# Turning six of eight halves' key sums by transposing DMAs over 16-bit planes instead of TensorE transposes

## The chip, the cores and the metric

The kernel runs on one core of one Trainium2 chip. The metric is device microseconds of one execution, as the median of several runs. The profile is a separate execution that the hardware profiler recorded.

## What is computed

Attention with positive random features (a softmax-free form) feeds a mixture of experts with one expert per token:

```python
# q, k, v: 8 batches x 8 heads x 576 tokens x 64; omega: 128 features x 64
q_s, k_s = (q * scale, k * scale)
def phi(x):
    h = einsum('bhsd,md->bhsm', x, omega) - sum(x * x, -1) / 2
    return exp(h - max(h, -1)) / sqrt(m)
kv  = einsum('bhsm,bhsd->bhmd', phi(k_s), v)      # sums over the keys
num = einsum('bhsm,bhmd->bhsd', phi(q_s), kv)
den = einsum('bhsm,bhm->bhs', phi(q_s), z) + 1e-06   # z: sum of phi(k_s)
x = (num / den) as 4608 tokens x 512
logits = normalised(x) @ normalised(expert_emb).T / tau
expert_idx = argmax(logits)                        # 8 experts
out[token] = gate * (relu(x @ w1[e]) @ w2[e])      # 512 -> 1024 -> 512
```

## The kernel before

The first stage, up to some 200 us, makes the attention and sorts the tokens by expert; the second, TensorE back to back, runs the experts. The change lies in the first.

It is one loop with 45 turns `i` over 36 token tiles of 128 rows. A super-batch has nine tiles and holds two batches, so that the key sums are made in eight halves (sb, b): a half is complete in turn 5, 9, 14, 18, 23, 27, 32 or 36. The queries run `LAG` = 7 turns behind the keys (`iq = i - LAG`). TensorE's order in a turn with both: projection of the queries (L373), transposes of the previous tile's query features (`qtr`, L461, into `nuu`), projection of the keys (L373), first step of the key sums `kv(1)` (L405), numerators `num` (L481, into `nuu`), second step `kv(0)` (L405). In words of the rows: `kva` holds key sums in accumulation memory, `kvs` their copy, `vtNv` the values of tile N, `ftk` and `ftq` the features, `xgp` a buffer of the second stage that is free here and lent out.

The routing logits need each head's key sums times the expert embeddings, eight more columns of `kvs`, so the numerator matmul of a query gives its logits too. For that the key sums must be turned around. Two turns after a half is complete, in the turning turn `i + 2`, which is 11, 16, 20, 25, 29 or 34 for the six middle halves, this happens:

- `kv_dense` (L423), still in turn i: GpSimd copies `kvs` into a dense 128x512 in `xgp[2]` (`xgp[NPRE]`).
- `kv_turn` (L432): four TensorE transposes of it, behind `kv(1)`.
- `kv_turned` (L436): VectorE copies the result back to `xgp[2]`.
- `kv_logits` (L443): 16 small matmuls with the embeddings, behind `num`, ahead of `kv(0)`. They write a strip of `nuu`'s second bank.
- `kv_logits_out` (L449): VectorE copies that strip into `kvs`, behind the emptying of the numerators (`num_out`, L494 to L500: `rr`, `lg`, `xr`). The next turn's `qtr` writes `nuu` again.

ScalarE makes the features (L387), copies half of the transposed queries (L466) and the key sums (L419). GpSimd does small steps of the routing (L520 to L593; from L589 on those that choose the first expert) and scatters finished tiles to memory with an indirect DMA (L569), one after the other. SP issues the loads of keys (L342), values (L357), queries (L363) and, from turn 29 on, of the first expert's weights (L601), and waits for buffers in that order. VectorE's and ScalarE's order is the order in which the code is written, by `todo` lists for named places in a turn; the other engines follow the scheduler's order.

Of the kernel before, what the change touches and what calls it, by code (L numbers as in the profile page):

```python
# [15 lines left out]
U16 = mybir.dt.uint16  # L16
# [7 lines left out]
B, H, S, D, M = 8, 8, 576, 64, 128  # L24
E, F = 8, 1024
N = B * S
DM = H * D
# [12 lines left out]
NPRE = 2  # L40
# [24 lines left out]
def attention_moe(ctx: ExitStack, tc: tile.TileContext, qT, kT, v1, omT, emb, tau, w1q, w2q, xs, out):  # L65
    nc = tc.nc
# [57 lines left out]
    xgp = [const.tile([P, PAY], F32, name=f"xgp{t}") for t in range(NPRE + 1)]  # L124
# [134 lines left out]
    def flush():  # L259
        while lows:  # L260
            lows.pop(0)()
# [60 lines left out]
    with ExitStack() as c1:  # L322
# [5 lines left out]
        kva, kvs, st = {}, {}, {}  # L328
# [5 lines left out]
        def load(i):  # L334

            if i >= NTILE:
                return
            if i == LAG - 1:
                st["k", i] = xgp[0][:, 0:DM].rearrange("p (c m) -> p c m", c=4)
            else:  # L340
                st["k", i] = p1.tile([P, 4, P], F32, name=f"kt{i}", tag="qt" if i in (2, 3) else "kt", bufs=2)
            nc.sync.dma_start(st["k", i], kT[i])  # L342
# [47 lines left out]
        def kvmm(i, a, b):  # L390
            sb, u = divmod(i, TPS)
            ft = st["fk", i, a]
            vt = st["v0", i] if (u, b) == (4, 0) else st["v", i]
            begin = u == 4 * b
            if begin:
                if (sb, b) == (0, 0):
                    kva[0, 0, a] = nu[a][:, 0 : 4 * (D + 1)].rearrange("p (h d) -> p h d", h=4)
                else:
                    kva[sb, b, a] = ps.tile([P, 4, D + 1], F32, name=f"kva{sb}_{b}_{a}", tag=f"kv{a}")
            acc = kva[sb, b, a]  # L400
            for h in range(4):


                for c in range(0, P, 64):
                    nc.tensor.matmul(  # L405
                        acc[c : c + 64, h, :], ft[:, h, c : c + 64], vt[:, 2 * h + a, :],
                        start=begin and h == 0, stop=u == 4 + 4 * b and h == 3,
                    )
            if u == 4 + 4 * b:
                if a == 0:  # L410
                    kvs[sb, b] = p1.tile([P, H, D + 1 + E], F32, name=f"kvs{sb}_{b}", tag="kvs", bufs=2)
# [22 lines left out]
        def kv_turned(sb, b):  # L434
            kvt = xgp[NPRE][:, 0:DM].rearrange("p (c m) -> p c m", c=4)
            nc.vector.tensor_copy(kvt.rearrange("p c m -> p (c m)"), st["kvb"])  # L436
            st["kvt", sb, b] = kvt

        def kv_logits(sb, b):
            st["kve", sb, b] = pe = nu[1][:, 424 : 424 + 8 * E].rearrange("p (c e) -> p c e", c=4)  # L440
            for c in range(4):
                for o in range(0, P, 64):
                    nc.tensor.matmul(  # L443
                        pe[o : o + 64, c], st["kvt", sb, b][:, c, o : o + 64], enbd[:, c].rearrange("p a e -> p (a e)"),
                        start=True, stop=True,
                    )
# [148 lines left out]
        def first_weights(n):  # L595

            if n == 0:
                st["fe"] = nc.values_load(firsti[0:1, NPRE + 1 :], engines=[ET.SP], min_val=0, max_val=E - 1, skip_runtime_bounds_check_because=WHY)
            q, wn = n // 2, ("w1", "w2")[n % 2]
            st["rf", n] = raw = rawp.tile([P, F], F32, name=f"rf{n}", tag=f"raw_{wn}")  # L600
            nc.sync.dma_start(raw, W[wn][0].rearrange("(e q) p f -> e q p f", q=NQ)[ds(st["fe"], 1), q].rearrange("o p f -> (o p) f"))  # L601
# [124 lines left out]
        early, spare, mid, ends, behind = {}, {}, {}, {}, []  # L726
# [9 lines left out]
        def go(d, *key):  # L736
            for f, *a in d.pop(key, ()):
                f(*a)
# [7 lines left out]
        for i in range(NTILE + LAG + 2):  # L746
# [3 lines left out]
            ahead = i + (4 if i < 2 else 2)  # L750
            if i < 2 or i > 4:
                load(ahead)
            if i in LOADS:
                first_weights(LOADS[i])
            if i == 1 or i >= 4:
# [10 lines left out]
            ks, qs = i < NTILE, 0 <= iq < NTILE  # L766
            st["both"] = ks
            sb, u = divmod(i - 1, TPS)

            def kv(*halves, b=None):  # L770
                if 0 <= i - 1 < NTILE:
                    for a in halves:
                        kvmm(i - 1, a, int(u > 4) if b is None else b)
# [5 lines left out]
            if ks and qs:  # L779
                if i > LAG:  # L780
                    proj(q1 + (3,), q0 + (1,))
                if turns:
                    qtr(iq - 1, *nu)
                maxima(*q1)
                if turns:
                    qcopy(iq - 1, 1)
                    qcopy(iq - 1, 0, True)
                maxima(*q0)
                go(spare, i, 4)
                feats(*q1)  # L790
                feats(*q0)
                proj(k1 + (2,), k0 + (0,))
                maxima(*k1)
                maxima(*k0)
                kv(1)
                if u == 4:
                    kv(0)
                    kv_out(sb, 0)
                go(spare, i, 3)
                slot(4)  # L800
                if sums:
                    num(iq - 1)
                go(spare, i, 0)
                go(spare, i, 1)
                slot(2)
                if u == 4:
                    kv(0, 1, b=1)
                else:
                    kv(0)
                if sums:  # L810
                    num_out(iq - 1)
                feats(*k1)
                feats(*k0)
                slot(0)
                slot(1)
            elif ks:
                for j in KPROJ.get(i, ()):
                    proj(*keys(j))
                if i == LAG - 1:
                    proj(("q", 0, 1, 3), ("q", 0, 0, 1))  # L820
                go(spare, i, 0)
                maxima(*k0)
                maxima(*k1)
                slot(0)
                if i == LAG - 1:
                    kv_out(0, 0)
                    kv_dense(0, 0)
                    for a in range(2):
                        kvmm(i - 2, a, 1)
                    kv_turn(0, 0)  # L830
                    emb2()
                kv(0, 1)
                slot(1)
                feats(*k0)
                go(spare, i, 1)
                feats(*k1)
                slot(2)
            else:
                mine, other = ((3, 1), (0, 2))[:: 1 if i % 2 == NTILE % 2 else -1]
                if qs:  # L840
                    proj(q1 + (mine[0],), q0 + (mine[1],))
                kv(1)
                go(spare, i, 2)
                slot(3)
                if turns:
                    qtr(iq - 1, *(pb[k] for k in other))
                kv(0)
                if sums:
                    num(done)
                go(spare, i, 0)  # L850
                if i == NTILE + 1:
                    flush()
                if qs:
                    maxima(*q1)
                    maxima(*q0)
                if i > NTILE and turns:
                    qcopy(iq - 1, 0, True)
                if qs:
                    feats(*q1)
                if i == NTILE:  # L860
                    kv_out(sb, 1)
                    qcopy(iq - 1, 0, True)
                if qs:
                    feats(*q0)
                if turns:
                    qcopy(iq - 1, 1)
                if sums:
                    num_out(done)
                flush()
                filled(1)  # L870
                slot(0)
                slot(1)
                filled(FILLS[i] - 1)
                go(spare, i, 1)
                slot(2)
            if sums and done % G == G - 1:
# [16 lines left out]
                for n, (d, *key) in enumerate(plan):  # L893
                    todo = at(d, *key) if key[0] < NTILE + LAG + 2 else behind
                    todo.insert(0 if n == 0 else len(todo), (next, steps, None))
            go(ends, i)
            if 0 <= i - 1 < NTILE and u in (4, 8):
                b = u // 4 - 1
                if b and ks:
                    kv_out(sb, b)  # L900
                k = int(not ks)
                if i + 2 == LAG:
                    todo = (kv_turned, spare, i + 2, 4), (kv_logits, spare, i + 2, 3), (kv_logits_out, mid, i + 2, 4)
                else:
                    kv_dense(sb, b)
                    todo = (kv_turn, spare, i + 2, 3 - k), (kv_turned, mid, i + 2, 4 - k)
                    todo += (kv_logits, spare, i + 2 + k, 0), (kv_logits_out, mid, i + 2 + k, 0)
                for f, *key in todo:
                    at(*key).append((f, sb, b))
# [184 lines left out]
    with tc.manual_schedule(engines={ET.PE, ET.Activation, ET.DVE, ET.Pool, ET.SP}):  # L1094
# [82 lines left out]
        for t in range(NPRE, NSTAT):  # L1177
# [10 lines left out]
            early = late and (t < SHIFT or t == ends)  # L1188
# [105 lines left out]
    with tc.If(tot > NSTAT):  # L1294
        with tc.For_i(NSTAT, tot, 1) as i:
            get = lambda k, eng, mx: nc.values_load(tabi[k : k + 1, ds(i, 1)], engines=[eng], min_val=0, max_val=mx, skip_runtime_bounds_check_because=WHY)
            xgl = x_of("x", get(0, ET.SP, DUM))
            src = get(2, ET.SP, E * NQ - 1)
# [65 lines left out]
```

## Time and profile before

| what | value |
|---|---|
| median of 3 runs | 637.44 us (637.18 to 638.03) |
| profiled execution | 641.91 us, of it span 640.3 us |
| TensorE busy | 627.2 us, 98% of the span |
| VectorE, ScalarE, GpSimd busy | 491.8, 431.8, 420.6 us |
| granted clock | 0.998 |

A row of the trace has the start in us from the start of the span and the duration; times of groups on TensorE overlap by the length of the pipeline, so a group's place is best read from its start to that of the next. The profiled execution is one run; it is not the median.

### The profile page before, as it was taken

How to read it: one execution, taken by the hardware profiler on the slowest of the kernel's cores; microseconds unless marked ns; L12 is line 12 of the kernel's file. 1: busy time of each engine (PE TensorE's matmuls, PEld its weight loads, DVE VectorE, ACT ScalarE, POOL GpSimd, SP SyncE). 2: the span in 40 equal slices, each digit the busy share in tenths (PEclk: the TensorE clock that was granted, in tenths of full speed). 3: DMA queues.
4: the chain of work that ended last, by engine and by line, in shares of the span. 5: the costliest groups of instructions: out<-in, count | busy, mean ns of one | idle time of the engine just before them, and what ended most of it. 6: DMA issues, size and time to landing. Idle time of an engine off the chain costs nothing.

```text
span 640.3 us, 19056 instructions
## 1 busy us (share of the span) xinstructions
PE 627.2 (98%) x6289; PEld 535.4 (84%) x6290; DVE 491.8 (77%) x908; ACT 431.8 (67%) x1139; POOL 420.6 (66%) x603
## 2 busy tenths in 40 slices
PE   9999999999999899999999999999999999999996
PEld 8899999988888688888888888888888888888885
DVE  5688888898879755687778887787778786878754
ACT  6898898898988426755666675757565756666630
POOL 3012443355777644569789797979797979798852
PEclk9999999999999999999999999999999999999999
DMA  7655664767772277978877788686869686878631
GB/s 255 199 153 163 216 209 154 233 203 229 271 270 100 101 239 275 264 183 242 210 237 200 210 232 245 185 256 172 245 184 236 208 237 200 229 218 216 201 116 46
DMA packets 142239, 131.93 MB, mean 206 GB/s; under 512 B 106742, under 2 KB 106870, under 8 KB 142144
## 3 DMA queue, kind: packets, MB, share of 16 engines
q1 hardware_dynamic: 135520, 109.70, 59.7%
q0 software_dynamic: 6480, 20.91, 8.4%
q8 instruction: 57, 0.93, 0.6%
q14 instruction: 38, 0.31, 0.2%
q10 hardware_dynamic: 144, 0.07, 0.0%
HBM read 83.78 MB, written 21.97 MB: 165 GB/s over the span
## 4 chain that ended last, share of the span: by engine, by line
PE 70%; ACT 2%; DVE 1%; DMA 1%; issue 0%; POOL 0%; ACTq 0%
PE pb L284 31%; PE po L284 31%; PE fs_o L284 2%; PE pb L373 1%; PE nuu L481 1%; ACT ftq L387 1%; PE pb L266 1%; PE fs_a L284 1%; DMA rf<-w2q 1%; PE kva L405 1%; PE pb L461 0%; DVE nmq L377 0%; DVE xr L500 0%; PE nuu L538 0%; PE nuu L461 0%
## 5 line engine op out<-in xcount | busy, mean ns | idle before, releaser
L239 POOL TENSOR_TENSOR w2l<-raww,w2h 128x256 f32 x128 | 143.3, 1120 | 7.6
L239 POOL TENSOR_TENSOR w1l<-raww,w1h 128x256 f32 (+1 forms) x130 | 112.5, 865 | 14.5 <-DMA xgp<-xs 5.2
L284 PE MATMUL po<-w2h,hh 128*128 (+1 forms) x288 | 112.2, 390 | 0.0
L284 PE MATMUL po<-w2h,hl 128*128 (+1 forms) x288 | 112.1, 389 | 0.0
L284 PE MATMUL po<-w2l,hh 128*128 (+1 forms) x288 | 112.1, 389 | 0.0
L284 PE MATMUL pb<-w1h,xh 128*128 (+1 forms) x280 | 109.4, 391 | 0.0
L284 PE MATMUL pb<-w1h,xl 128*128 (+1 forms) x280 | 109.0, 389 | 0.0
L284 PE MATMUL pb<-w1l,xh 128*128 (+1 forms) x280 | 109.0, 389 | 0.0
L1084 DVE COPY pl<-pb 128x512 uint16<-128x512 uint16 x68 | 46.7, 689 | 60.2 <-ACT pl L1080 55.9
L1080 ACT ACTIVATE pl<-pb 128x512 uint16<-128x512 uint16 x68 | 39.4, 585 | 76.3 <-PE pb L284 66.5
L314 POOL DMA_INDIRECT y<-xgp,tail x36 | 45.0, 1250 | 55.2 <-DVE w1h L233 28.8
L387 ACT ACTIVATE ftq<-pb,nmq 128x128 f32<-128x128 f32 x288 | 79.6, 429 | 2.2 <-DVE nmq L377 1.3
L387 ACT ACTIVATE ftk<-pb,nmk 128x128 f32<-128x128 f32 x272 | 76.6, 479 | 6.0 <-DVE nmk L377 4.3
L1102 DVE COPY wd<-t 128x1024 uint16<-128x1024 uint16 x68 | 65.4, 963 | 1.6 <-DMA t<-pl 1.5
L1118 ACT ACTIVATE hh<-wd 128x1024 fp32r<-128x1024 f32 x34 | 36.1, 1063 | 42.7 <-DVE wd L1102 38.1
L284 PEld LDWEIGHTS po<-w2h,hh 128*128 128x128 f32 x288 | 54.1, 188 | 11.2
L284 PEld LDWEIGHTS po<-w2l,hh 128*128 128x128 f32 x288 | 54.1, 188 | 11.2
L284 PEld LDWEIGHTS po<-w2h,hl 128*128 128x128 f32 x288 | 54.0, 187 | 11.2
L284 PEld LDWEIGHTS pb<-w1h,xl 128*128 128x128 f32 x280 | 52.6, 188 | 11.0
L284 PEld LDWEIGHTS pb<-w1l,xh 128*128 128x128 f32 x280 | 52.6, 188 | 10.9
L284 PEld LDWEIGHTS pb<-w1h,xh 128*128 128x128 f32 x280 | 52.5, 187 | 10.7
L1122 DVE SCALAR_TENSOR_TENSOR hl<-wd,hh 128x1024 fp32r<-128x1024 f32 x34 | 54.2, 1594 | 4.0 <-ACT hh L1118 3.4
(341 smaller groups left out, 1250.4 us busy)
## 6 DMA issues: line engine op xcount, KB each, us to landing
raww<-w1q SPq DMA_DIRECT2D x38, 512.0 KB
raww<-w2q SPq DMA_DIRECT2D x38, 512.0 KB
qt<-qT SPq DMA_DIRECT2D x36, 256.0 KB
kt<-kT SPq DMA_DIRECT2D x35, 256.0 KB
xg<-xs SPq DMA_DIRECT2D x23, 260.5 KB
xgp<-xs SPq DMA_DIRECT2D x15, 260.5 KB
rf<-w1q SPq DMA_DIRECT2D x4, 512.0 KB
rf<-w2q SPq DMA_DIRECT2D x4, 512.0 KB
```

Source lines behind the costliest of these rows:

```text
L239: ils.append(eng.tensor_tensor(at(l, d)[:, c], raw[:, c], at(h, d)[:, c].bitcast(F32), op=ALU.subtract))
L266: nc.tensor.transpose(bank[:, c * P : (c + 1) * P], src[:, o + c * P : o + (c + 1) * P], ident)
L284: done.append(nc.tensor.matmul(dst, x[:, c * P : (c + 1) * P], ws.rearrange("p o f -> p (o f)"), start=(begin and i == 0 and k == 0), stop ...
L314: w = nc.gpsimd.indirect_dma_start(out=out, out_offset=bass.IndirectOffsetOnAxis(ap=(xg[:, DM:] if tail is None else tail)[:, E : E + 1].b ...
L373: nc.tensor.matmul(st["pj" + w, i, a][:, c, :], st[w, i][r, c, :], om[r, :], start=True, stop=True)
L387: nc.scalar.activation(ft[:, h, :], pj[:, h, :], AF.Exp, bias=nm[:, h : h + 1])
L405: nc.tensor.matmul(acc[c : c + 64, h, :], ft[:, h, c : c + 64], vt[:, 2 * h + a, :], start=begin and h == 0, stop=u == 4 + 4 * b and h == 3,)
L1080: nc.scalar.activation(planes[1][:, o : o + 512], halved(src)[:, :, 1], AF.Copy)
L1084: nc.vector.tensor_copy(planes[0][:, o : o + 512], halved(src)[:, :, 0])
L1102: nc.vector.tensor_copy(to, src)
L1118: nc.scalar.activation(hh, wd[:, 0:F], AF.Relu)
L1122: nc.vector.scalar_tensor_tensor(hl, wd[:, 0:F], 0.0, hh.bitcast(F32), op0=ALU.max, op1=ALU.subtract)
```

## The change

For the six middle halves, while keys are still loaded, the turn of the 32-bit sums is made from two 16-bit halves of each value. `kv_planes` lets GpSimd take `kvs` apart into two planes, low and high 16 bits, in `xgp[2]`, in turn i. `kv_spun` has SP issue two DMA transposes, one per plane, into `xgp[0]`, in turn i + 1, ahead of the values' load. `kv_joined` lets GpSimd join the planes to 32-bit values in `xgp[2]`, in turn i + 2. `kv_logits` goes to a new place, behind `kv(0)` and ahead of the emptying; `kv_logits_out` keeps its own. The first half and the last stay as they were. Lines of the changed kernel behind L438 are 18 higher.

```diff
+        def kv_planes(sb, b):
+            pl = xgp[NPRE][:, 0:DM].bitcast(U16).rearrange("p (k c a d) -> p k a c d", k=2, a=2, d=D)
+            src = kvs[sb, b].bitcast(U16).rearrange("p (a c) (w two) -> p a c w two", a=2, two=2)
+            for k in range(2):
+                nc.gpsimd.tensor_copy(pl[:, k], src[:, :, :, 0:D, k])
+
+        def kv_spun(sb, b):
+            pl = xgp[NPRE][:, 0:DM].bitcast(U16).rearrange("p (k f) -> p k f", k=2)
+            st["t16", sb, b] = xgp[0][:, 0:DM].bitcast(U16).rearrange("p (k c m) -> p k c m", k=2, c=4)
+            for k in range(2):
+                nc.sync.dma_start(st["t16", sb, b][:, k], pl[:, k], transpose=True)
+
+        def kv_joined(sb, b):
+            st["kvt", sb, b] = kvt = xgp[NPRE][:, 0:DM].rearrange("p (c m) -> p c m", c=4)
+            to = xgp[NPRE][:, 0:DM].bitcast(U16).rearrange("p (c m two) -> p c m two", c=4, two=2)
+            for k in range(2):
+                nc.gpsimd.tensor_copy(to[:, :, :, k], st["t16", sb, b][:, k])
+
@@
                 load(ahead)
+            go(early, i, "spin")
             if i in LOADS:
@@
                     kv(0)
+                go(spare, i, 2)
                 if sums:
@@
+                elif ks:
+                    kv_planes(sb, b)
+                    todo = (kv_spun, early, i + 1, "spin"), (kv_joined, mid, i + 2, 4)
+                    todo += (kv_logits, spare, i + 2, 2), (kv_logits_out, mid, i + 2, 0)
                 else:
                     kv_dense(sb, b)
```

TensorE at the end of turn 11, before: the transposes stand behind `kv(1)` (`vt10v` with the first feature half), the numerators repeat, and the logits stand ahead of `kv(0)`.

```order
L405 MATMUL kva_0_1_883<-vt10v,ftk_1_924 64x65 x8
L432 MATMUL pb_74<-ident,xgp_137 128x128 x4
L481 MATMUL nuu<-kvs_0_439,qp_0_976 64x73
...
L443 MATMUL nuu<-enbd,xgp_137 64x16 x8
L405 MATMUL kva_0_0_908<-vt10v,ftk_0_929 64x65 x8
L373 MATMUL pb_74<-om,qt_823 128x128
```

The same place in the changed program:

```order
L405 MATMUL kva_0_1_886<-vt10v,ftk_1_927 64x65 x8
L499 MATMUL nuu<-kvs_0_439,qp_0_979 64x73
...
L405 MATMUL kva_0_0_911<-vt10v,ftk_0_932 64x65 x8
L461 MATMUL nuu<-enbd,xgp_137 64x16 x8
L373 MATMUL pb_74<-om,qt_824 128x128
```

The transposes are gone, and the logits have gone from ahead of `kv(0)` to behind it, right ahead of the next turn's projection.

GpSimd from the end of turn 14 into turn 16, before (`xgp_137` is `xgp[2]`, L569 the scatter, L547 to L557 routing steps):

```order
L423 COPY xgp_137<-kvs_0_1392 128x2x4x64
L489 COPY xr_1555<-ids 128x1
L547 TENSOR_TENSOR base_1572<-base_1572,run 128x24
...
L557 TENSOR_TENSOR pos_1576<-pos_1576 128x3
L569 DMA xs<-xr_917,posi_1280 38016x576
L563 CAST posi_1681<-pos_1576 128x3
```

The same place in the changed program (`xgp_135` is `xgp[0]`):

```order
L443 COPY xgp_137<-kvs_0_1392 128x2x4x64 x2
L507 COPY xr_1558<-ids 128x1
L565 TENSOR_TENSOR base_1575<-base_1575,run 128x24
...
L575 TENSOR_TENSOR pos_1579<-pos_1579 128x3
L587 DMA xs<-xr_920,posi_1280 38016x576
L455 COPY xgp_137<-xgp_135 128x512 x2
L581 CAST posi_1673<-pos_1579 128x3
```

One copy has become two, and two joins stand behind the scatter of turn 16.

GpSimd in turn 29, before:

```order
L593 TENSOR_TENSOR keyc<-keyc,iote 128x8
L563 CAST posi_3251<-pos_3114 128x3
L520 TENSOR_TENSOR t_3255<-lg_2971 128x96
L521 TENSOR_TENSOR t_3255<-t_3255 128x3x16
L522 TENSOR_TENSOR raw_3253<-t_3255 128x24
L569 DMA xs<-xr_2587,posi_3251 38016x576
L489 COPY xr_3376<-ids 128x1
```

The same place in the changed program:

```order
L611 TENSOR_TENSOR keyc<-keyc,iote 128x8
L581 CAST posi_3254<-pos_3114 128x3
L538 TENSOR_TENSOR t_3258<-lg_2971 128x96
L539 TENSOR_TENSOR t_3258<-t_3258 128x3x16
L540 TENSOR_TENSOR raw_3256<-t_3258 128x24
L587 DMA xs<-xr_2587,posi_3254 38016x576
L455 COPY xgp_137<-xgp_135 128x512 x2
L507 COPY xr_3376<-ids 128x1
```

Here the joins stand behind the last step of choosing the first expert (L611), three sums of the routing and the scatter.

## Rows read from the trace of the kernel before

**Rows 1.** Windows: us, then busy of PE, PEld, DVE, ACT, POOL; clock, DMA share, GB/s

```profile
31.44:175.78 144.34, 143.18 (x3165) 131.98 (x3161) 124.30 (x298) 128.37 (x464) 61.29 (x178) 1.00 0.65 204
240.00:600.00 360.00, 359.75 (x1603) 297.65 (x1602) 276.90 (x372) 229.68 (x462) 290.47 (x283) 1.00 0.77 221
```

**Rows 2.** Timeline of PE in turn 11: start, us, engine, line, what, [idle before <-releaser]

```profile
44.26 0.69 PE L405 MATMUL kva<-vt10v,ftk 128*64 128x65 f32 x16
44.87 0.66 PE L432 MATMUL pb<-ident,xgp 128*128 128x128 f32 x4
45.46 1.25 PE L481 MATMUL nuu<-kvs,qp 128*64 128x73 f32 x32
46.54 0.59 PE L443 MATMUL nuu<-enbd,xgp 128*64 128x16 f32 x16
...
48.69 0.53 PE L461 MATMUL nuu<-ident,ftq 64*128 64x64 f32 x10
```

**Rows 3.** Timeline of DVE in turn 11

```profile
47.25 0.17 DVE L494 TENSOR_SCALAR rr<-nuu 128x8 f32<-128x8 f32 x1 [0.62 <-PE nuu L443]
...
48.42 0.21 DVE L449 COPY kvs<-nuu 128x64 f32<-128x64 f32 x1
```

**Rows 4.** Waits, 31.44 to 175.78: who <- whom: total us, times, longest

```profile
ACT qp L466 <- PE nuu L461: 12.3, 12, 2.4
DVE rr L494 <- PE nuu L443: 4.4, 6, 0.8
```

**Rows 5.** Timeline of PE in turn 13, a turn without transposes

```profile
55.38 0.69 PE L405 MATMUL kva<-vt12v,ftk 128*64 128x65 f32 x16
...
57.49 0.72 PE L373 MATMUL pb<-om,qt 64*128 64x128 f32 x8
```

**Rows 6.** Timeline of PE: kv(1) and logits of turns 16, 20 (logits), 29

```profile
71.46 0.69 PE L405 MATMUL kva<-vt15v,ftk 128*64 128x65 f32 x16
...
73.76 0.65 PE L443 MATMUL nuu<-enbd,xgp 128*64 128x16 f32 x16
...
95.61 0.59 PE L443 MATMUL nuu<-enbd,xgp 128*64 128x16 f32 x16
...
142.88 0.69 PE L405 MATMUL kva<-vt28v,ftk 128*64 128x65 f32 x16
...
145.40 0.62 PE L443 MATMUL nuu<-enbd,xgp 128*64 128x16 f32 x16
```

**Rows 7.** Timeline of POOL: scatter of turn 16, copy of turn 18's half, scatter of turn 29

```profile
71.52 1.04 POOL L569 DMA_INDIRECT xs<-xr,posi  x1 [0.54 <-issue]
...
89.28 0.62 POOL L423 COPY xgp<-kvs 128x512 f32<-128x512 f32 x1
89.84 0.19 POOL L563 CAST posi<-pos 128x3 int32<-128x3 f32 x1
...
144.46 1.06 POOL L569 DMA_INDIRECT xs<-xr,posi  x1 [0.50 <-DVE nmk L377]
```

**Rows 8.** Groups of POOL, 31.44 to 180: count | busy, mean ns | idle before

```profile
L616 POOL TENSOR_TENSOR w1l<-rf,w1h 128x256 fp32r<-128x256 f32 x10 | 7.0, 725 | 0.1
L423 POOL COPY xgp<-kvs 128x512 f32<-128x512 f32 x6 | 3.7, 622 | 18.2 <-ACT kvs L419 18.1
```

**Rows 9.** Groups of ACT by form, 250 to 620

```profile
L1104 ACT ACTIVATE wd<-t 128x512 uint16<-128x512 uint16 x58 | 41.0, 777 | 0.0
L1116 ACT ACTIVATE xh<-wd 128x512 fp32r<-128x512 f32 x29 | 18.2, 626 | 0.0
```

**Rows 10.** Timeline of SP's queue and DVE around one pair of transposes

```profile
254.85 2.71 SPq L1090 DMA_TRANSPOSE t<-pl  x2
...
259.13 0.76 DVE L1102 COPY wd<-t 128x1024 uint16<-128x1024 uint16 x1 [0.30 <-DMA t<-pl]
```

**Rows 11.** Timeline of SP's queue and ACT: weights of turn 33

```profile
167.49 1.02 SPq L601 DMA_DIRECT2D rf<-w1q  x1
...
175.54 1.24 ACT L607 ACTIVATE w1h<-rf 128x1024 fp32r<-128x1024 f32 x1
```

## The prediction

> **What bounds the kernel now.** I read the stage of the change first, as one window: of its 144.34 us TensorE is busy 143.18, and in the later expert stage it is busy 359.75 of 360 [rows 1]. Nothing there can take up a delay, so what the first stage loses or wins reaches the end whole. Every instruction taken from TensorE seems to pay, but the change touches only six loop turns (11, 16, 20, 25, 29, 34, "turning turns"), so I read these one by one.
>
> In turn 11 TensorE runs the second key-sum step kv(1) at 44.26, the four transposes at 44.87 (0.59 to the next group at 45.46), the numerators, the routing logits L443 at 46.54, kv(0), the next turn's projection, and the query transposes L461 at 48.69 [rows 2]. VectorE's row beside it tells more than TensorE's: L494, the first step of emptying the numerators, has waited 0.62 us for L443, though the numerators are done, and the copy of the logits L449 ends the emptying at 48.42 + 0.21 = 48.63, 0.06 before L461 starts [rows 3]. L494 has such a wait for L443 six times, once per turning turn (4.4 us), and ScalarE has its own largest wait for L461 (12.3 us) [rows 4]. So there is a chain through the turning turn: **logits start, emptying on VectorE, L461, ScalarE's query copy**. From the start of the logits to L461 it takes 48.69 - 46.54 = 2.15 us, and the other five turns read the same within 0.07. What the change moves is therefore not TensorE's time; it is the moment when the logits start.
>
> **The change part by part.** Per half (six of eight) it removes four transposes (0.59), VectorE's copy L436 and one GpSimd copy; it adds two GpSimd copies ("planes") at the end of turn i, two transposing DMAs on SP in turn i+1, two GpSimd copies ("joins") in turn i+2, and puts the logits behind kv(0). In the order of the changed program L494 still waits for the last logits matmul, so the chain is the same with a new starting point.
>
> *TensorE.* A turn without transposes goes from kv(1) to the next turn in 57.49 - 55.38 = 2.11 us, kv(0) included [rows 5]. The logits now stand at that end, so they start no earlier than 2.11 us behind kv(1). Before, they started 46.54 - 44.26 = 2.28 behind it (turns 11 and 20), 73.76 - 71.46 = 2.30 in turn 16 [rows 2, 6], and 2.34 to 2.36 in 34 and 25. The transposes give 0.59 back, but kv(0), now ahead of the logits, takes most of it. What is won at best is 0.17 (11), 0.17 (20), 0.19 (16), 0.25 (25), 0.23 (34), and in turn 29 2.52 - 2.11 = 0.41, where the transposes had waited for GpSimd: 1.42 us in all, against 6 x 0.59 = 3.5 of TensorE's time. That is where a reading of TensorE alone goes astray.
>
> *GpSimd, the joins.* TensorE's logits need both joins. On GpSimd, which runs in order, the joins stand behind a scatter in the turning turns (the order shows it). In turn 16 the scatter ends at 71.52 + 1.04 = 72.56 [rows 7]. A copy of 128x512 costs 0.62 by the mean of the removed line [rows 8], with 0.56 from its start to the next instruction's (89.28 to 89.84, a repeat in the other five). Two joins take 0.56 + 0.62 = 1.18, then 0.06 to reach TensorE as above: logits at 73.80, against 73.76 before: +0.04, and the 0.19 are gone. Turns 25 and 34 repeat this pattern with scatters that end 1.18 and 1.24 before the old logits: +0.06 and 0.00. In turn 29 the scatter ends late, at 144.46 + 1.06 = 145.52, behind a row of small operations that choose the first expert; the old logits had started at 145.40 [rows 6, 7]. With 1.24 behind it they start at 146.76: **+1.36**. In turns 11 and 20 GpSimd is through in time: -0.17 each. Sum at 0.62 a copy: 0.04 + 0.06 + 0 + 1.36 - 0.34 = +1.12 us.
>
> The price of a join has no row: it writes 16-bit values with gaps. ScalarE's joins of the same kind take 777 ns against 626 for its plain 128x512 [rows 9], a factor of 1.24; on GpSimd that would be 0.77 each. I take 0.70, between 0.62 and 0.77: 0.16 more per pair in the four turns that wait, +0.64. **Sum +1.76, say +1.8 us.** At 0.77 it is 1.12 + 1.2 = +2.3. Bounds: were a copy priced by its bytes, 0.40 (0.19, what a cast of three elements takes [rows 7], plus half of the rest), a pair is 0.75, turns 11, 16, 20, 25 and 34 win all they can (-1.01) and 29 loses 0.93: -0.1. At the price of the two-input L616, (0.72 - 0.19) / 256 = 2.1 ns an element [rows 8], a copy takes 1.25 and a pair 2.44: 1.26 more in each of four turns, and turn 20 joins in by about 2.5: +8.6.
>
> The Trainium skill, GPSIMD Engine Reference, section Elementwise — side-by-side cycle accounting, counts the loop per element and not per byte: 1.03 cycles for a one-input body, 768 ns for 512 elements in a slower loop. The 0.62 of the row lies between what these two would make; by the slower one the sum would be the +2.3 above, and by either the bound by bytes falls.
>
> *The planes* are one copy more than before (0.56) at the end of turn i, with GpSimd mostly waiting behind; where a scatter is already late behind it, it shifts that by at most 0.56. I cost it at nothing, with four times 0.1 in the range.
>
> *The DMAs.* The nearest row is a pair twice as wide, issued at 254.85, whose second half VectorE reads at 259.13: 4.28 us from issue to use [rows 10]. Tightest is turn 20: planes from 89.28, first issue at about 90.0, landed by 94.3, joined by 95.5, against a logits start of 95.61 before [rows 6, 7]. At 0.70 a join it may lose its 0.17; the other five halves have more. DMA engines are busy 0.65 of the stage [rows 1]. On SP the two issues (2.71 for the wide pair) stand behind the key load, and wait there for GpSimd's planes; behind them are value and query loads and, in turn 33, the first expert's weights: issued at 167.49, read by ScalarE from 175.54 [rows 10, 11]. Some 2 us later they are still in time: nothing.
>
> The Trainium skill, VectorE: DVE Perf Modes, section The three transpose paths, sets 390 ns on TensorE against 1309 by DMA for 128x128, and the rules section below it says to use TensorE if a PSUM destination is fine. That speaks against this change; the rows agree in direction (0.59 for four transposes against microseconds by DMA), but here the DMA has a turn of cover, so the rule alone alters no term above.
>
> *VectorE.* L436 ran in time in which VectorE would wait at L494 anyway [rows 3]: nothing.
>
> The profiled execution has 641.91 with a span of 640.3, so 1.6 lie outside; the median of the runs is 637.44, 4.5 lower. I add the sum to either: 639.2 by the median, some 643.7 for a profiled run with a span of 642.1.
>
> **The rivals.** *A, the forecast*: one turn, 29, costs over a microsecond, three are level to slightly late, two win a little: 638.3 to 640.6.
> *B, GpSimd's copies are cheap, or its scatter in turn 29 comes earlier because the planner's small operations move.* The joins then come as TensorE does: from the full 1.42 won to the 0.1 of the price by bytes, with a little lost: 636.0 to 638.3. Against it: a cast of three elements takes 0.19 already [rows 7], so halving the bytes halves little.
> *C, the chain does not bind* and TensorE's freed time is returned: 6 x 0.59 = 3.5, **633.9, faster.** It decides if L461 could start without the emptying; against it speaks the 0.06 between L449 and L461 and the same 2.15 to 2.22 six times over.
> *D, 16-bit copies cost as two-input ones, or the DMA lands late*: each waits in every turning turn; it decides from about 1 us a copy, or 5 us for a pair: 641 to 646.
> That the DMAs do not replace the transposes is excluded: in the changed order the TensorE rows are gone.
>
> **How the numbers follow.** A 0.48, D 0.18, B 0.24, C 0.10. About 0.2% (1.27 us) is what a measurement of this kernel can tell from no change: same is 636.17 to 638.71. Of A some 0.08 lies inside it, of B nearly all (0.22, with 0.02 faster): faster 0.12, same 0.30, slower 0.58. The likeliest is A at 639.2. The range 636.0 to 642.5 takes in B, all of A and the near part of D.
>
> **What would show it.** Right: in the changed trace the logits of turn 29 wait for GpSimd's join, 1.2 us or more behind the scatter, and L461 some 2.15 after the logits; turns 11 and 20 a little shorter; two joins of 0.6 to 0.8 each; no wait of the joins for DMA. Wrong: joins of 0.4 or of over 1 us, joins that wait for the transposes, or a turn whose L461 starts less than 2 us behind its logits.

## The result, and the profile after

The changed kernel takes 645.35 us (median of 7 runs, 644.25 to 651.21) against 637.44 for the kernel before: 7.9 us slower where I had said 1.8. The ratio over all runs is 1.0138, 95% interval 1.0112 to 1.0164. The profiled execution is one of the long ones: 649.54 us, of it a span of 647.8. One caution for everything below: the kernel before takes 637 to 638 us on some chips and 641.9 on others, so each ratio is against runs of it on the same chip, and the rows ahead of the prediction come from an execution as long as the second kind, 641.91.

First the waits of the changed kernel's first stage, 31 to 180 us (who waits for whom: total us, times, longest). Lines are 18 higher here, so L512 is the first step of the emptying (L494 before) and L461 is the logits (L443 before); in the kernel before, L461 is the query transposes.

```profile
DVE rr L512 <- PE nuu L461: 13.4, 5, 3.8
PEld nuu L461 <- POOL xgp L455: 7.5, 4, 2.6
PE nuu L461 <- POOL xgp L455: 6.9, 4, 2.5
POOL xgp L455 <- DMA xgp<-xgp: 4.6, 4, 1.4
```

The order of things is the one of the prediction: VectorE's emptying waits for the logits (13.4 us, where it was 4.4 in [rows 4]), the logits for GpSimd's joins (L455), and the joins, which I had not expected, for the DMA. The price of a copy is nearly what I took (GpSimd, 31.44 to 190 us: count | busy, mean ns | idle before):

```profile
L455 POOL COPY xgp<-xgp 128x512 uint16<-128x512 uint16 x12 | 8.5, 755 | 4.6 <-DMA xgp<-xgp 4.6
L443 POOL COPY xgp<-kvs 128x512 uint16<-128x512 uint16 x12 | 7.0, 617 | 18.1 <-ACT kvs L419 18.0
```

A plane costs what the 32-bit copy cost ([rows 8], 622 ns), a join 755 ns, between the 0.70 and the 0.77 of the prediction. So not the price of a copy but the time at which things came was wrong. Turn 25 on the queue of SP, on GpSimd and on TensorE:

```profile
116.72 2.87 SPq L449 DMA_TRANSPOSE xgp<-xgp  x2
```

```profile
121.74 1.04 POOL L587 DMA_INDIRECT xs<-xr,posi  x1 [0.54 <-issue]
124.13 1.42 POOL L455 COPY xgp<-xgp 128x512 uint16<-128x512 uint16 x2 [1.35 <-DMA xgp<-xgp]
```

```profile
121.24 0.69 PE L405 MATMUL kva<-vt24v,ftk 128*64 128x65 f32 x16
121.76 1.19 PE L499 MATMUL nuu<-kvs,qp 128*64 128x73 f32 x32
122.79 0.63 PE L405 MATMUL kva<-vt24v,ftk 128*64 128x65 f32 x16
125.60 0.80 PE L461 MATMUL nuu<-enbd,xgp 128*64 128x16 f32 x16 [2.18 <-POOL xgp L455]
126.33 2.08 PE L373 MATMUL pb<-om,qt 64*128 64x128 f32 x16
```

The transposes are issued at 116.72 and the join starts at 124.13, 7.4 us later and 1.35 after the scatter ahead of it. The logits then start 125.60 - 121.24 = 4.36 behind kv(1). And one more thing is new: the projection behind them takes 2.08, where the one behind the logits of turn 16 takes 1.16. In turn 29 no DMA is waited for; there GpSimd itself is late:

```profile
142.08 1.18 POOL L443 COPY xgp<-kvs 128x512 uint16<-128x512 uint16 x2
...
147.63 1.06 POOL L587 DMA_INDIRECT xs<-xr,posi  x1 [0.50 <-DVE raw L543]
148.70 1.43 POOL L455 COPY xgp<-xgp 128x512 uint16<-128x512 uint16 x2
```

```profile
145.55 0.69 PE L405 MATMUL kva<-vt28v,ftk 128*64 128x65 f32 x16
...
150.18 1.04 PE L461 MATMUL nuu<-enbd,xgp 128*64 128x16 f32 x16 [2.46 <-POOL xgp L455]
151.15 2.08 PE L373 MATMUL pb<-om,qt 64*128 64x128 f32 x16
```

Logits 4.63 behind kv(1), again with a projection of 2.08. Windows of the changed kernel show what stands behind these two rows (us, then busy of PE, PEld, DVE, ACT, POOL; TensorE's granted clock, DMA share, GB/s):

```profile
69.00:70.00 1.00, 1.00 (x27) 0.99 (x27) 0.73 (x3) 0.74 (x3) 0.62 (x3) 1.00 5.16 178
70.00:71.00 1.00, 1.00 (x20) 0.88 (x20) 1.00 (x3) 0.99 (x3) 0.61 (x3) 1.00 0.28 13
71.00:72.00 1.00, 1.00 (x30) 0.92 (x31) 1.00 (x3) 1.00 (x5) 0.63 (x1) 1.00 0.07 16
...
126.00:129.00 3.00, 3.00 (x42) 2.96 (x40) 1.89 (x6) 0.00 (x0) 0.90 (x3) 0.50 0.28 101
150.00:157.00 7.00, 6.82 (x90) 6.56 (x92) 4.83 (x13) 2.87 (x11) 1.76 (x7) 0.52 0.56 204
184.00:187.00 3.00, 2.81 (x32) 2.63 (x32) 2.02 (x5) 1.65 (x6) 2.40 (x5) 0.50 0.75 255
```

In turn 16 the transposes are issued at 66.36. At 69 to 70 the DMA share reads 5.16, more than a share can be; I read that as packets that began there and took long. Then the queues moved 13 and 16 GB/s for two microseconds. Behind the waits of turns 25, 29 and 34 the granted clock is 0.50, that is 1.2 of 2.4 GHz, for 3 to 7 us.

### The profile page after: what moved, and what is told of

It is laid out like the page before. It is cut to its first block, busy times and chain, and to the rows that moved or that the text cites. A ratio compares the mean times of both kernels' runs of the same rounds, so it can differ in the third digit from the quotient of the medians.

```text
span 647.8 us, 19059 instructions
## 1 busy us (share of the span) xinstructions
PE 624.4 (96%) x6265; PEld 535.6 (83%) x6266; DVE 489.1 (75%) x902; ACT 433.2 (67%) x1139; POOL 432.2 (67%) x621
## 4 chain that ended last, share of the span: by engine, by line
PE 83%; DMA 5%; POOL 4%; DVE 4%; ACT 2%; issue 2%; SPq 1%; POOLq 0%; DVEq 0%; ACTq 0%
PE pb L284 31%; PE po L284 30%; PE pb L373 7%; PE nuu L499 3%; PE kva L405 3%; DMA xgp<-xgp 2%; PE nuu L479 2%; DMA rf<-w2q 2%; PE fs_o L284 2%; POOL xgp L455 1%; DVE xr L518 1%; PE pb L266 1%; PE nuu L405 1%; POOL xs L587 1%; PE nuu L461 1%
## 5 line engine op out<-in xcount | busy, mean ns | idle before, releaser
L1126 DVE COPY wd<-t 128x1024 uint16<-128x1024 uint16 x68 | 66.7, 983 | 1.1 <-DMA t<-pl 1.1
```

Of the source, the lines that this page charges most:

```text
L1126: nc.vector.tensor_copy(to, src)
```

## The experiments

**Two controls.** The kernel before, unchanged, for a second profile:

> The kernel before, unchanged, for a second profile. Its profiled execution took 641.9 against a median of 637.4. Theory: that execution was a long one, and a second one lies within 1.5 of the median, 637 to 639; then the turns' starts of both profiles show how far one profile may be trusted. Rival: recording always costs some 4 us: 641.5 to 642.

Measured: 638.26 (ratio 1.001, 0.9999 to 1.0021); the profiled execution took 637.38, span 635.7. So recording does not cost 4 us, and the rival falls. The execution that I had read was a long one; on the chips of the longer kind all executions of this kernel are (641.2 or more). In the second, turn 16 on TensorE and on GpSimd reads:

```profile
70.56 0.69 PE L405 MATMUL kva<-vt15v,ftk 128*64 128x65 f32 x16
...
73.06 0.59 PE L443 MATMUL nuu<-enbd,xgp 128*64 128x16 f32 x16
```

```profile
71.06 1.05 POOL L569 DMA_INDIRECT xs<-xr,posi  x1 [0.54 <-issue]
```

kv(1) comes 0.9 earlier than in [rows 6], the scatter only 0.46 earlier: it ends 1.55 behind kv(1), not 1.10 as in [rows 6, 7]. TensorE had been late in the first profile, and that hid part of GpSimd's lateness: turn 15, by the starts of kv(1), took 5.57 us there and 5.04 here. Which of the two a profile shows goes with the kind of chip. Turn 15 took 5.51 to 5.57 in all four profiles below from chips on which the kernel before takes 641.9, and 5.02 to 5.05 in all others but one (5.50 with the planes on ScalarE). So I had added a sum with the phase of the long kind to the median of the short kind.

The changed kernel a second time:

> The changed kernel unchanged, for a second profile. Its first profiled execution took 649.5, with the clock at 0.987; the median of its runs is 645.35. Theory: the landing of the DMA and the clock behind the waits differ from one execution to the next, the waits in turns 29 and 34 do not: profile between 644 and 647, logits of turn 29 again 4.6 us and of turn 34 3.5 to 4 us behind kv(1), those of 16, 20 and 25 anywhere between 2.5 and 4.4. Rival: all waits repeat within 0.1 us.

Measured, on a chip where the kernel before takes 641.91: 648.03, ratio 1.0097 (1.0079 to 1.0114), span 646.5, clock 0.994. So on this chip the change costs 6.1 us. The profile lies a little above the range that I gave (648.2), which I had set by the other kind of chip. The logits started 2.01, 2.62, 3.47, 3.75, 4.37 and 2.59 behind kv(1) in the six turns; turn 34, which I had called constant, was not.

From here on I read every kernel in one way: the start of the logits behind kv(1) in the six turns. Each number is the difference of two rows like those above; the last line sums what each is later than the second profile of before. Each column is one execution.

| turn | before | changed | no DMA | fed | joins on VectorE |
|---|---|---|---|---|---|
| 11 | 2.28 | 2.01 | 2.01 | 2.00 | 2.08 |
| 16 | 2.50 | 4.26 | 3.04 | 3.94 | 2.57 |
| 20 | 2.28 | 2.75 | 2.01 | 3.11 | 2.37 |
| 25 | 2.50 | 4.36 | 3.05 | 4.36 | 2.56 |
| 29 | 2.54 | 4.63 | 4.16 | 4.63 | 3.42 |
| 34 | 2.50 | 3.77 | 3.28 | 3.99 | 2.64 |
| sum over before | | +7.2 | +3.0 | +7.4 | +1.0 |

**The chain: one part of the change alone.**

```diff
+                go(spare, i, 2)
@@
-                    todo += (kv_logits, spare, i + 2 + k, 0), ...
+                    todo += (kv_logits, spare, i + 2 + k, 0 if k else 2), ...
```

> The kernel before with one part of the change alone: the logits stand behind kv(0) instead of ahead of it; transposes, VectorE's copy and GpSimd's copy stay, no planes, no DMA. Theory 1 (the chain from the start of the logits through VectorE's emptying to the next query transposes sets the pace of a turning turn): the logits start later by kv(0), 0.43 to 0.56 us, in six turns, and everything behind is later by as much: 2.6 to 3.4 us over the kernel before, some 640.4. Rival (TensorE's own work sets the pace, and the order of two steps in it is free): 637.4, within 0.5.

Measured: 640.56, ratio 1.0046 (1.0031 to 1.0060): 2.7 us slower for the order of two steps. TensorE in turn 11:

```profile
43.92 0.69 PE L405 MATMUL kva<-vt10v,ftk 128*64 128x65 f32 x16
...
46.67 0.60 PE L443 MATMUL nuu<-enbd,xgp 128*64 128x16 f32 x16
47.19 1.16 PE L373 MATMUL pb<-om,qt 64*128 64x128 f32 x16
48.83 0.71 PE L461 MATMUL nuu<-ident,ftq 64*128 64x64 f32 x16 [0.47 <-DVE kvs L449]
```

From logits to the query transposes, L461, it is 2.16 us, as before, and L461 now waits 0.47 for the emptying. Each of the six turns is 0.46 to 0.51 longer by the starts of kv(1), 2.9 us in sum, and between them little changes (turn 24 is 0.23 longer). The chain is shown, and that a shift passes on nearly whole.

**The landing of the DMA.**

```diff
-            pl = xgp[NPRE][:, 0:DM]...
+            pl = xgp[0][:, 0:DM]...
@@
-            for k in range(2):
-                nc.sync.dma_start(st["t16", sb, b][:, k], pl[:, k], transpose=True)
```

> The changed kernel without its transposing DMAs: GpSimd writes the planes straight to where the joins read them, so the logits use sums that were not turned around. All GpSimd copies stay. Theory 2 (late landing is half of the loss): the joins' waits for the DMA, 1.25 us in turn 16, 1.35 in turn 25, 0.57 at TensorE in turn 20, are gone, and the halved clock behind turn 25 with them (0.9): 3 to 4 us under the changed kernel, 641.3 to 642.3; TensorE's wait in turn 29 (2.5 us) stays. Rival (GpSimd's order alone): within 1 us of the changed kernel, 644.5 to 646.

Measured: 773.14, a time that says nothing: with sums that were not turned the tokens go to other experts, and the second stage has other work. I had not thought of that. The first stage can be read. TensorE in turns 25 and 29:

```profile
120.23 0.69 PE L405 MATMUL kva<-vt24v,ftk 128*64 128x65 f32 x16
...
123.28 0.65 PE L458 MATMUL nuu<-enbd,xgp 128*64 128x16 f32 x16 [0.87 <-POOL xgp L452]
...
142.75 0.69 PE L405 MATMUL kva<-vt28v,ftk 128*64 128x65 f32 x16
...
146.91 0.66 PE L458 MATMUL nuu<-enbd,xgp 128*64 128x16 f32 x16 [1.99 <-POOL xgp L452]
```

The scatter of turn 29 on GpSimd:

```profile
144.36 1.07 POOL L584 DMA_INDIRECT xs<-xr,posi  x1 [0.50 <-DVE nmk L377]
```

Turn 20 wins its 0.27, 16 and 25 lose 0.55 instead of 1.8, and 29 keeps most of its loss. Of the 7.2 us of the profile of after, 4.2 are gone without the DMA: 3.3 in turns 16, 20 and 25, where the joins had waited for the landing, and 1.0 in turns 29 and 34, where no join waited for it and GpSimd itself now comes 0.5 earlier. The other 3.0 stay.

**Turn 29.**

```diff
-                elif ks:
+                elif ks and (sb, b) != (2, 1):
```

> The changed kernel with the one half that is turned in turn 29 left on TensorE as before; five halves by DMA. Theory 3 (turn 29, behind the choice of the first expert on GpSimd, is the costliest half): its 2.3 us of late logits and the 2.1 of halved clock behind them are gone: 4 us or more under the changed kernel, 640.9 to 641.4. Rival (the loss is spread evenly over the halves): one sixth to one fifth of 7.9 less, 643.8 to 644.

Measured: 643.35, ratio 1.0086 (1.0071 to 1.0101): 5.5 us over the kernel before on its chip instead of 7.9, so some 2.4 us less, not 4. By the starts of kv(1) turn 29 is now 0.35 longer than in the second profile of before, instead of 4.0. So it was the costliest, but 1.9 of those 4.0 are clock, which the other executions have to a different degree.

**The clock.**

```diff
+        def fed(n):
+            for _ in range(n):
+                nc.tensor.transpose(pb[3][:, 0:P], ident, ident)
@@
+                    if i + 2 in (16, 25, 29, 34):
+                        at(spare, i + 2, 2).append((fed, 10))
```

> The changed kernel with ten more transposes of the identity on TensorE (about 1.5 us, their result unused) between kv(0) and the logits in turns 16, 25, 29 and 34, where TensorE waits 1.6 to 2.5 us for the joins. Theory 4 (part of the loss is the clock that is at half behind these waits): granted clock stays 1.00 in the stretches behind turns 25 and 29, the runs lie closer together, 2 to 4 us under the changed kernel: 641.5 to 643.4. Rival (the clock falls for another reason, or costs nothing because TensorE would wait there anyway): 645, within 1, with the same halved stretches.

Measured: 645.73 (644.97 to 646.44), ratio 1.0126 (1.0111 to 1.0140), again 7.9 us over the kernel before: no faster than the changed kernel. TensorE in turn 29:

```profile
146.42 1.31 PE L453 MATMUL pb<-ident 128*128 128x128 f32 x10
148.94 0.65 PE L465 MATMUL nuu<-enbd,xgp 128*64 128x16 f32 x16 [1.21 <-POOL xgp L459]
149.52 1.16 PE L373 MATMUL pb<-om,qt 64*128 64x128 f32 x16
```

The clock does stay up (projection 1.16, mean 0.999), and the runs lie within 1.5 us instead of 7; but the median did not fall. In this profile the lateness alone, 7.4 by the table, makes nearly all of the 7.9 of the measurement. In the first profile of after the turns grew by 11.4, of which 7.2 is lateness and 4.1 the halved clock (0.9 behind turn 25, 1.9 behind 29, 1.3 behind 34); in the second by 6.9 over [rows 2, 6], with 4.7 and 2.2. What the clock costs in the median run stays open: the landing differs so much from one execution to the next that the two can't be parted. The mean granted clock of every run is on record, though: 0.987 to 0.990 in the three executions of the changed kernel above 646 us, 0.993 to 0.995 in the four from 644.25 to 645.35. So the clock goes with the long executions; the median, held against the fed kernel's, hardly shows it.

**Joins on VectorE.**

```diff
-                nc.gpsimd.tensor_copy(to[:, :, :, k], st["t16", sb, b][:, k])
+                nc.vector.tensor_copy(to[:, :, :, k], st["t16", sb, b][:, k])
```

> The changed kernel with the joins on VectorE, where the removed copy stood, instead of GpSimd. Theory (GpSimd's queue and its joins make the logits of turns 29 and 34 late, the landing of the DMA those of 16 and 25): TensorE's waits for the logits fall from 2.5 and 1.6 us to nothing in turns 29 and 34 and stay at 1 us or more in 16 and 25; 640.5 to 642.5. Rival A (the landing makes nearly all of the loss): 643.5 to 645.5. Rival B (it is all GpSimd's queue): 637 to 638.5.

Measured: 641.05, ratio 1.0055 (1.0034 to 1.0076): 3.0 us over the kernel before on its chip instead of 7.9. VectorE in turn 29:

```profile
143.55 1.03 DVE L455 COPY xgp<-xgp 128x512 uint16<-128x512 uint16 x2 [0.59 <-issue]
```

A pair takes 0.8 to 0.9 there in the other turns. Turns 16, 25 and 34 are within 0.15 of before, since the join no longer stands behind the scatter and in this execution the DMA had landed. Theory and size hold for GpSimd's part; that 16 and 25 would go on waiting 1 us or more did not. The table leaves 1.0 us, the measurement 3.0. By the starts of kv(1) this profile has lost 0.4 ahead of turn 11 and 0.7 in turns 22, 23, 28 and 32, beside the 1.3 of the six turns, all against the second profile of before; why, I can't say.

**Planes on ScalarE too.**

```diff
-                nc.gpsimd.tensor_copy(pl[:, k], src[:, :, :, 0:D, k])
+                nc.scalar.activation(pl[:, k], src[:, :, :, 0:D, k], AF.Copy)
```

> The changed kernel with the planes on ScalarE, right behind its copy of the key sums, and the joins on VectorE; GpSimd has no part in it. Theory (the planes come late because GpSimd is behind, and the DMA lands late for that): SP issues the transposes 1 to 2 us earlier, the waits for the landing fall below 0.5 us each, and what is left is 1.2 us more of ScalarE in each of six turns: 638.5 to 641. Rival (the transposes are slow to land wherever they start): like the kernel with the joins alone on VectorE, or above it.

The joins stand on VectorE as in the run above; the cut shows the other part of the edit. Measured: 642.56, ratio 1.0071 (1.0054 to 1.0087), above the range. ScalarE at the end of turn 9:

```profile
37.92 0.80 ACT L419 ACTIVATE kvs<-kva 128x260 f32<-128x260 f32 x2
38.81 1.17 ACT L443 ACTIVATE xgp<-kvs 128x512 uint16<-128x512 uint16 x2
39.89 0.57 ACT L484 ACTIVATE qp<-nuu 128x512 f32<-128x512 f32 x1
```

The two planes stand ahead of the query copy that the next numerators need, and turn 10 is 1.3 us longer, turns 19 and 32 by 1.2 and 1.1. The logits start 2.0 to 2.8 behind kv(1), in sum 0.9 earlier than before. The transposes are issued only 0.4 earlier in turns 16 and 25, where they stand behind the key load, and the joins there still wait 0.57 and 0.69 for the landing, a little more than the theory allowed. ScalarE has no 1.2 us to give there.

**The side work by itself.**

```diff
+                    if ks:
+                        kv_planes(sb, b)
+                        at(early, i + 1, "spin").append((kv_spun, sb, b))
```

> The kernel before with the planes on GpSimd and the transposing DMAs added as side work whose result nobody reads; TensorE's transposes, the copies and the order of the logits stay. It prices what I had put at nothing. By my prediction: 637.4 to 638.2. Rival (two more GpSimd copies and twelve transposing DMAs delay scatters and loads that others wait for): 639 to 642.

The two functions are those of the change, with the planes in `xgp[1]`. Measured: 638.82 against 638.03, ratio 1.0011 (1.0001 to 1.0021), so 0.8 us, 0.6 above the range. Planes and DMAs that nobody waits for cost about a tenth of the 7.9. The loss is in waiting for them.

**Transposes ahead of the loads, twice.**

```diff
+            go(early, i, "spin")
             for n in QLOADS.get(...): loadq(n)
             load(ahead)
-            go(early, i, "spin")
```

> The changed kernel with SP issuing the two transposes ahead of the query and the key load of their turn instead of behind them. In turns 16 and 25 they landed 7.3 us after their issue, behind these loads, and in 11 and 20, with emptier queues, 4.1 to 4.3. Theory (they land late because the loads issued just ahead of them still fill the DMA queues): the joins' waits for the landing in 16, 20 and 25 (1.25, 0.79, 1.35) fall by at least half, 2 to 3 us under the changed kernel, 642 to 643.5. Rival A (the transposes stall by themselves, whatever is ahead): waits as before, 644.5 to 646. Rival B (SP, now waiting for GpSimd's planes, holds up the loads): above 646.

> The kernel with the transposes ahead of the loads, a second time: in its first profiled execution TensorE lost 3.3 us in the first eight turns, where its instructions are those of the changed kernel, by a key load that came late. Theory: the turning turns cost what they did (logits 2.0, 2.6, 2.6, 2.7, 4.7 and 2.6 us behind kv(1)), some 4 us over the kernel before on the same chip, so 1 to 3 us under the changed kernel's 7.5 more. Rival (SP held up by the planes delays loads): again more than the changed kernel.

Measured: 650.66 (646.03 to 653.6), ratio 1.0128 (1.0093 to 1.0163), 8.8 us over the kernel before on that chip and 2.6 over the changed kernel there; and 646.54, ratio 1.0072 (1.0056 to 1.0088), 4.7 us over the kernel before on another chip. Two medians of one kernel that differ by 4 us don't tell whether the order helps. The first profile has lost 3.3 us in the first eight turns, where the program is that of the changed kernel (TensorE waits 1.89 for a key load). SP and GpSimd in turn 25 of the second:

```profile
115.45 3.14 SPq L449 DMA_TRANSPOSE xgp<-xgp  x2
```

```profile
121.29 1.04 POOL L587 DMA_INDIRECT xs<-xr,posi  x1 [0.54 <-DMA xgp<-xgp]
122.34 1.44 POOL L455 COPY xgp<-xgp 128x512 uint16<-128x512 uint16 x2
```

The join follows the scatter at once, in turns 16 and 25 of both executions (logits 2.6 and 2.7 behind kv(1)). Turn 20, where SP waits for the planes in either order, still waits 1 us. But this is not a quicker landing shown. The transposes of turn 25 are now issued 5.7 us ahead of kv(1) instead of 4.5 and 4.1 in the two profiles of the changed kernel: 1.2 and 1.5 us more lead, against waits of 1.35 and 1.08 that went. Where the joins still wait, in turns 11 and 20, it is 4.0 to 4.6 from issue to use, against 4.1 to 5.4 in those two. And turn 16 had no wait in the second of them either. The rival, loads held up behind the transposes, shows in one place: in turn 21 of the second profile TensorE waits 0.92 for a query load.

**All of it together**: transposes ahead, joins on VectorE, turn 29's half on TensorE.

> The best that the runs point to: transposes ahead of the loads, joins on VectorE, and the half of turn 29 left on TensorE; five halves by DMA. Theory: the logits then start 2.1 to 2.6 us behind kv(1), against 2.3 to 2.5 before, no turn gains or loses more than 0.3: within 1 us of the kernel before, no gain to speak of, because VectorE's join ends no earlier than the copy that it replaces. Rival (the freed 0.59 us of TensorE per half come back once nothing is late): 2.5 to 3 us under the kernel before.

Measured: 643.01 against 641.88 on the same chip, ratio 1.0023 (1.0000 to 1.0045). TensorE and VectorE in turn 16:

```profile
72.85 0.69 PE L405 MATMUL kva<-vt15v,ftk 128*64 128x65 f32 x16
...
74.96 0.65 PE L461 MATMUL nuu<-enbd,xgp 128*64 128x16 f32 x16
```

```profile
74.00 0.81 DVE L455 COPY xgp<-xgp 128x512 uint16<-128x512 uint16 x2
...
75.71 0.17 DVE L512 TENSOR_SCALAR rr<-nuu 128x8 f32<-128x8 f32 x1 [0.90 <-PE nuu L461]
```

Now nothing is late: the logits start 2.11 behind kv(1), as TensorE alone would have it in [rows 5], and 0.13 to 0.20 earlier than in the profile ahead of the prediction in all five turns. That is nearly the whole gain that a half can have with the logits behind kv(0), 0.9 us in sum against some 3 of TensorE's time. The measurement does not show it; in the profile the six turns are 0.8 us shorter in sum, and 1.5 us are lost in the first eight turns, where the programs are the same. No version beat the kernel before.

## Why the prediction was wrong

- **The sign and the chain held.** The chain from the logits through VectorE to L461 sets the pace (2.7 us for the move alone), TensorE's freed time is not returned (rival C falls), turn 11 wins 0.27, the joins behind the scatter of turn 29 cost most. My own sign of being wrong came true: joins that wait for the transposes, 4.6 us. Rival D, "the DMA lands late", had 641 to 646; I gave it 0.18.
- **The step that failed: the landing.** I wrote that turn 20 was the tightest and "the other five halves have more". I had the price from one row, a pair in the second stage [rows 10], 4.28 us. Turns 11 and 20 confirm it in the first profile (4.3 and 4.1), but in 16 and 25 it was 7.3 and 7.4, and the joins waited. I had looked at the mean DMA share of the stage (0.65) and not at the microseconds around the issue. This term was put at nothing and is 3.3 of the profile's 7.2 us (turns 16, 20 and 25).
- **GpSimd's time of arrival, mis-sized.** I took 1.10 us from kv(1) to the end of the scatter in turn 16, from an execution in which TensorE was itself late. In the second profile it is 1.55, and before's logits are at 2.50 instead of 2.30: the net is 0.2 to 0.35 more in each of turns 16, 25 and 34. Without any DMA the table gives +3.0, where I had said +1.8; the rest is mainly the pair of joins at 1.43 (I took 1.34).
- **"The planes at nothing".** In turn 29 the scatter ends 3.14 behind kv(1), 2.68 in the second profile of before; in turn 34 2.29 against 1.61. The second plane alone does not do that: the kernel without DMA has the same planes and ends the scatter of turn 29 at 2.68. There the scatter ahead of the planes ended 4.03 before kv(1), in the kernel before 3.93, in the changed one 3.48, and GpSimd then had no break left to take the plane up. What turns 29 and 34 lose beyond the run without DMA is 1.0 us of the 7.2; in the second profile the scatter of turn 34 was on time (1.09). I had seen the condition and put it into the range, not into the sum.
- **A term that was missing: the clock.** No row of before has a granted clock below 1.00 in this stage, and I asked nowhere what a wait of over 2 us on TensorE would do to the work behind it. By the growth of the turns beyond the lateness it cost 4.1 us in one profile and 2.2 in another, both of long executions; in the median it stays open.
- **What else was costed at nothing.** The traffic and the planes by themselves came to some 0.8 us. No run parts VectorE's removed copy from the rest. The loads behind the transposes were not quite nothing: ScalarE waits 0.51 and 1.30 us in the two profiles of the changed kernel for weights of the first expert, which it never did before, and turn 32 is 0.5 and 1.4 longer. How much of that reaches the end is not shown.
- The Trainium skill, VectorE: DVE Perf Modes, section Rules for kernel authors, says to turn a 128x128 block on TensorE where a PSUM destination is fine. The runs agree for this place: no version with DMA transposes beat the kernel before. The Trainium skill, GPSIMD Engine Reference, section Elementwise — side-by-side cycle accounting, counts GpSimd's loop per element. By that a 16-bit copy would cost as much as a 32-bit one of as many elements; the planes' 617 against 622 ns agree.

## What to carry to other kernels

Removing work from the busiest engine pays only as far as the chain that meets it at the next hand-over gets earlier; find the instruction that ends the wait there and ask when it starts, not how long the engine works. A transfer put in place of work has to be priced at its landing with the queues as they are in that microsecond, and as a spread rather than one number. And a phase between two engines read from one profile is worth a second profile before a sum is built on 0.2 us of it.

## What the runs showed of the hardware that I had not expected

- A pair of 128x512 16-bit DMA transposes took 4.1 to 7.4 us from issue to use where the use waited for it, in the four profiles with the change's order on SP and joins on GpSimd: 4.1 to 5.4 in turns 11 and 20, 6.3 to 7.4 in 16 and 25. The two 256 KB loads (query and key) just ahead do not part them, for in the first profile they are issued 0.4 and some 2 us ahead in turn 11 as in turn 25. What differs is how busy the DMA engines were by the profile: a share of 0.57 to 0.72 over the 4 us ahead of the issue in turns 11 and 20, 0.84 to 0.92 in 16 and 25. That the one causes the other is not shown. Turns 11 and 25 of the first profile:

```profile
35.75:39.75 4.00, 4.00 (x90) 3.74 (x88) 3.43 (x9) 4.00 (x17) 1.00 (x2) 1.00 0.58 162
112.72:116.72 4.00, 4.00 (x101) 3.81 (x98) 3.50 (x11) 3.51 (x14) 2.42 (x6) 1.00 0.92 283
```

- On GpSimd a 128x512 16-bit copy takes 617 ns reading with gaps and 755 ns writing with gaps, against 622 for 32-bit values; on VectorE a pair of the joins takes 0.8 us, on GpSimd 1.43.
- The clock. Behind TensorE's waits of 2.18 and 2.46 us (turns 25 and 29) it was at 1.2 GHz for 3 to 7 us; behind 1.72 us in turn 16 it was not (projection 1.16 at 75.71). In the kernel without DMA it fell in turn 16 behind a shorter wait:

```profile
73.43 0.65 PE L458 MATMUL nuu<-enbd,xgp 128*64 128x16 f32 x16 [0.86 <-POOL xgp L452]
...
76.51 2.02 PE L373 MATMUL pb<-om,kt 64*128 64x128 f32 x16
```

So the length of one wait does not tell whether the clock falls.
